# Threshold search on distances, conversion words in PSUM, dummy products in the first choice, three low halves from SBUF

## The chip, the core and the metric

The kernel runs on one core of a Trainium2 chip. The metric is the device time of one execution in microseconds (us). Engines are TensorE (PE; its weight loads are shown as PEld), VectorE (DVE), ScalarE (ACT), GpSimd (POOL) and SyncE (SP).

## The reference

Attention with a gated bias on 4 x 8 heads of 576 x 64, then a layer of eight experts in which the (token, expert) pairs are taken by falling logit until each expert has 288 of the 2304 tokens, then a dense layer with a mish-like activation.

```python
attn_out = _attn_ref(**attn_kwargs)              # causal, bias from a running sum of max(s, 0)
x = attn_out.transpose(0, 2, 1, 3).reshape(B * S, H * D)
logits = x @ w_gate; order = np.argsort(-logits.flatten())
for idx in order:
    tok, e = idx // E, idx % E
    if assigned[tok] >= 0 or counts[e] >= cap: continue
    assigned[tok] = e; counts[e] += 1
out[mask] = np.maximum(x[mask] @ w1[e], 0.0) @ w2[e]      # for each expert e
h = x @ w_in
return ((h * np.tanh(np.log1p(np.exp(h)))) @ w_out).astype(np.float32)
```

`w_in` and `w_out` arrive as 64-bit floats; the kernel reads them as pairs of 32-bit words.

## The kernel before, in words

All products are made in three: each operand is a high part of reduced precision and a low part, the rest.

*Attention* (lines 664 to 1106) works through 224 blocks in a fixed order. `t_unit` transposes queries and keys (a tail of 64 rows at L795), `guard` (L877) bounds the scores, `emit_s` makes scores, `emit_pv` the value products (L983 to L985; key block 4 has 64 rows), and `post_pair` turns results back and adds up the gate logits `L`.

*Conversion* (class `Convert`, from L31). The 64-bit weights of the dense layer come in 64 units of 128 x 256. Each takes three DVE steps that join the two words into one float (L101, L104, L107, one per `yield`), then a high part on ACT (L83) and a low part on POOL (L84). 21 units are converted during attention into tiles that the experts use later, and are split later by `settle`. The others have a tile named `c1` (six buffers), which the activation `mish` shares. `conv(n)` takes n steps.

*The choice* (`route(e)`, L254) finds the expert that is next full and its 288 tokens. `m` is each token's best logit. A threshold is found in six searches, two of 64 candidates and four of 32: a mask on DVE (L263), 18 products that count per expert (L268), a comparison with 288 that counts thresholds (L272), a diagonal (L274) and a product that spreads the counts over all partitions (L276), a maximum (L279), and a few small operations on integer keys for the next candidates (L288 to L309). Then come counts (L328), the expert (L338), ranks (L350, L351), a one-hot per slot (L373), products that gather the token numbers (L378), and an indirect DMA of the tokens (L391). Everything of it that lies in PSUM lies in one bank, `bank` (named `rt` in the trace).

For expert 0 this runs by itself between attention and the experts: at each `yield` the loop at L640 takes conversion steps by the list `BUB`, settles three units, and once the expert is known loads and splits its weights (`feed`, L435: loads by SP, high part on ACT L431, low part on POOL L432). For experts 1 to 7 it runs beside the expert before: `step()`, called after every third product, counts down the number that `route` yielded.

*The experts.* `up(e)` makes 192 products (w1, relu, w2) and `down(e)` 384 on the dense layer, in 16 blocks f. `mish` follows each first-layer product: L555, four ACT operations (L556 to L559), then `product` (L562) four ticks later, ACT (L564), and `low` (L568) one tick later. The product banks `hp` are three; the second layer lags by three blocks. `make_xt` (L489) transposes the gathered tokens. In `up` and `down` one conversion step is taken per tick (two ticks per twelve products) until all are done; `need` takes more if a unit is missing.

```python
    BUB = []
    for T in range(6):
        BUB += [2 if T < 1 else 4 if T < 2 else 2, 1, 2, 0]
    BUB += [2, 3, 2, 0, 1, 0] + [0] * (NT // 6 + 1) + [4]
    BUB9 = 6
```

By these lists the first choice takes 32 steps in its searches, 12 behind them, and 6 before `make_xt(0)`.

Of the kernel before, what the change touches and what calls it, by code (L numbers as in the profile page):

```python
# [27 lines left out]
def fb(ap):  # L28
    return ap.bitcast(F32)


class Convert:


    def __init__(self, nc, w_in, w_out, ring):
# [5 lines left out]
        self.limit, self.loaded, self.done, self.raw, self.held = 0, 0, 0, {}, []  # L41
        self.steps = self.run()
# [47 lines left out]
    def run(self):  # L90
        nc = self.nc
        for i, unit in enumerate(self.units):
# [4 lines left out]
            if self.wide:  # L97
# [6 lines left out]
                nc.vector.scalar_tensor_tensor(a, w[:, :, :, 1], -0x40000000, a, op0=OP.bitwise_and,  # L104
                                               op1=OP.bitwise_or)
                yield
                nc.vector.scalar_tensor_tensor(a, w[:, :, :, 0], 29, a, op0=OP.logical_shift_right,  # L107
# [10 lines left out]
def constants(nc, one, K):  # L118
# [12 lines left out]
    nc.gpsimd.memset(new("onesb", [128, 128], BF16), 1.0)  # L131
    yield
# [21 lines left out]
    jj, th1, j20 = K["jj"], new("th1", [128, 64], I32), new("j20", [128, 64], F32)  # L154
    x1 = j20.bitcast(I32)
    nc.vector.tensor_scalar(th1, jj, -32.0, float(2 ** 26), op0=OP.add, op1=OP.mult)
    yield
    nc.vector.tensor_scalar(x1, th1, 31, 0x7FFFFFFF, op0=OP.arith_shift_right, op1=OP.bitwise_and)
    yield
    nc.vector.tensor_tensor(th1, th1, x1, op=OP.bitwise_xor)  # L160
    yield
    nc.vector.tensor_copy(th1[:, 0:1], th1[:, 1:2])
    yield
    nc.vector.tensor_scalar(j20, jj, float(2 ** 20), None, op0=OP.mult)
    yield
# [45 lines left out]
def experts(ctx, tc, K, ring, ident, L, x_dram, w1, w2, cv, out):  # L211
# [14 lines left out]
    jj, onesb, upper, slots, aux, erow, th1, j20, cb = (K[n] for n in (  # L226
        "jj", "onesb", "upper", "slots", "aux", "erow", "th1", "j20", "cb"))
    steps = K["steps"]
# [4 lines left out]
    diag = one.tile([128, E], F32R, name="diag")  # L233
    nc.gpsimd.memset(fb(diag), 0.0)
# [4 lines left out]
    place = {}  # L239

    def inbank(name, n):
        if name not in place:
            place[name] = place.get("", 144)
            place[""] = place[name] + n
            assert place[""] <= 512
# [899 lines left out]
```

## Time and profile before

| | |
|---|---|
| runs | 1065.06, 1066.26, 1062.24 us; median 1065.06 |
| profiled execution | 1061.81 us, its span 1059.9 us |
| busy | PE 957.4 us (90%), DVE 675.5, ACT 627.7, POOL 437.1 |
| granted PE clock, mean | 0.948 of full speed (2.4 GHz) |
| chain that ended last | PE 62%, DVE 13%, issue 9%, ACT 6%, DMA 5%, POOL 3% |

Busy times are shares of one profiled execution. In a row of the timeline the first number is the start in us from the span's begin, the second the duration; in square brackets stands how long the engine was idle before, and what ended that. "x18" means that so many neighbouring instructions are merged, and the duration is that of all.

### The profile page before, as it was taken

Reading aid. Unit: us, or ns where it says so; the run is one execution under the profiler, and the core shown is the slowest. Engines: PE = TensorE matmul, PEld = TensorE weight load, DVE = VectorE, ACT = ScalarE, POOL = GpSimd, SP = SyncE. Lnnn points to the kernel's source line nnn. Section 1 sums busy time; section 2 is a strip of 40 time slices with the busy share of each in tenths; the row PEclk is TensorE's granted clock in tenths of the full one; section 3 lists DMA queues with packets and bytes.
Section 4 is the critical chain, followed back from the end, with each engine's and each line's share of the span. In section 5 each row is a group of like instructions: output and inputs, shape, how many; then the busy total and the mean of one; then the engine's idle time right before and its main releaser. Section 6 shows DMA issues by size and latency. Waiting matters only on the chain.

```text
span 1059.9 us, 21486 instructions
## 1 busy us (share of the span) xinstructions
PE 957.4 (90%) x7625; PEld 919.4 (87%) x7625; DVE 675.5 (64%) x2041; ACT 627.7 (59%) x1405; POOL 437.1 (41%) x441
## 2 busy tenths in 40 slices
PE   6899988999923879899999999999999999999996
PEld 5788877888812779899998999999999999999996
DVE  7767787997688789746645645655664664443243
ACT  4667765777741357646745664664674565575563
POOL 5546666567665652460251045036035115502401
PEclk8889998999965899999999999999999999999998
DMA  5898999893234534330230123123033023401200
GB/s 131 177 192 194 211 194 204 193 211 96 63 119 140 156 108 127 97 104 1 85 99 22 51 71 86 40 63 103 1 98 108 1 61 98 139 11 30 74 1 23
DMA packets 134580, 105.58 MB, mean 100 GB/s; under 512 B 63977, under 2 KB 114313, under 8 KB 134441
## 3 DMA queue, kind: packets, MB, share of 16 engines
q1 hardware_dynamic: 122520, 83.50, 32.3%
q10 hardware_dynamic: 8880, 11.27, 3.5%
q0 software_dynamic: 3072, 9.44, 2.8%
q8 instruction: 60, 0.98, 0.4%
q14 instruction: 48, 0.39, 0.1%
HBM read 69.55 MB, written 9.73 MB: 75 GB/s over the span
## 4 chain that ended last, share of the span: by engine, by line
PE 62%; DVE 13%; issue 9%; ACT 6%; DMA 5%; POOL 3%; SPq 1%; ACTq 0%; POOLq 0%; DVEq 0%
PE y L462 8%; PE hp L462 8%; PE y L463 7%; PE y L464 7%; PE hp L463 7%; PE hp L464 7%; PE pv L983 2%; PE t L1028 2%; PE s L945 2%; DMA qkraw<-in_k_dram 2%; PE t L877 2%; POOL wt L432 2%; PE pv L985 2%; PE pv L984 1%; PE rt L268 1%
## 5 line engine op out<-in xcount | busy, mean ns | idle before, releaser
L432 POOL TENSOR_TENSOR wt<-raw,wt 128x512 fp32r<-128x512 f32 x128 | 164.2, 1299 | 368.9 <-ACT wt L431 355.3
L962 POOL TENSOR_TENSOR Pl<-P,Ph 128x384 fp32r<-128x384 f32 (+2 forms) x128 | 137.0, 1077 | 98.6 <-DVE Ph L961 45.1
L462 PE MATMUL hp<-xu,WI 128*128 128x288 f32 x512 | 154.5, 302 | 14.8 <-DVE act L568 14.8
L462 PE MATMUL y<-act,WO 128*128 128x288 f32 x512 | 156.6, 306 | 0.0
L464 PE MATMUL hp<-xu,WI 128*128 128x288 f32 x512 | 152.0, 297 | 0.0
L463 PE MATMUL y<-act,WO 128*128 128x288 f32 x512 | 151.9, 297 | 0.0
L464 PE MATMUL y<-act,WO 128*128 128x288 f32 x512 | 151.6, 296 | 0.0
L463 PE MATMUL hp<-xu,WI 128*128 128x288 f32 x512 | 151.1, 295 | 0.4 <-DVE xu L540 0.4
L562 DVE SCALAR_TENSOR_TENSOR hp<-c,hp 128x288 f32<-128x288 f32 x128 | 58.8, 459 | 86.5 <-ACT c L559 85.1
L462 PEld LDWEIGHTS hp<-xu,WI 128*128 128x128 f32 x512 | 96.6, 189 | 16.9 <-DVE act L568 16.9
L431 ACT ACTIVATE wt<-raw 128x512 fp32r<-128x512 f32 x128 | 79.7, 625 | 41.2 <-DMA raw<-in_moe_w_dram 18.0
L463 PEld LDWEIGHTS hp<-xu,WI 128*128 128x128 f32 x512 | 97.1, 190 | 0.9 <-DVE xu L540 0.9
L463 PEld LDWEIGHTS y<-act,WO 128*128 128x128 f32 x512 | 97.6, 191 | 0.0
L464 PEld LDWEIGHTS y<-act,WO 128*128 128x128 f32 x512 | 97.2, 190 | 0.0
L462 PEld LDWEIGHTS y<-act,WO 128*128 128x128 f32 x512 | 97.0, 190 | 0.0
L464 PEld LDWEIGHTS hp<-xu,WI 128*128 128x128 f32 x512 | 96.7, 189 | 0.0
L555 DVE TENSOR_SCALAR c<-hp 128x288 f32<-128x288 f32 x128 | 58.2, 455 | 58.2 <-PE hp L464 46.6
L522 DVE SCALAR_TENSOR_TENSOR act<-hp,act 128x288 fp32r<-128x288 f32 x64 | 29.2, 456 | 101.3 <-ACT act L521 100.6
L556 ACT ACTIVATE c<-c 128x288 f32<-128x288 f32 x128 | 56.7, 443 | 60.2 <-DVE c L555 58.2
L954 ACT ACTIVATE P<-s 128x384 f32<-128x384 f32 (+2 forms) x128 | 63.9, 504 | 40.7 <-PE s L947 23.5
L564 ACT ACTIVATE act<-hp 128x288 fp32r<-128x288 f32 x128 | 52.3, 408 | 60.0 <-DVE hp L562 56.8
L462 PE MATMUL hp<-xu,wt 128*128 128x288 f32 x256 | 80.8, 315 | 1.4 <-ACT xu L499 1.4
(230 smaller groups left out, 2790.1 us busy)
## 6 DMA issues: line engine op xcount, KB each, us to landing
raw<-in_moe_w_dram SPq DMA_DIRECT2D x128, 256.0 KB
QKB<-qk SPq DMA_DIRECT2D x55, 288.0 KB
QKA<-qk SPq DMA_DIRECT2D x29, 288.0 KB
r<-in_moe_w_out_dram ACTq DMA_DIRECT2D x22, 256.0 KB
r<-in_moe_w_in_dram ACTq DMA_DIRECT2D x21, 256.0 KB
qkraw<-in_q_dram SPq DMA_DIRECT2D x32, 128.0 KB
qkraw<-in_k_dram SPq DMA_DIRECT2D x32, 128.0 KB
vraw<-in_v_dram SPq DMA_DIRECT2D x32, 128.0 KB
```

What stands on the lines that cost most here:

```text
L431: nc.scalar.activation(t[:, 0], r, AF.Copy)
L432: nc.gpsimd.tensor_sub(t[:, 1], r, fb(t)[:, 0])
L462: nc.tensor.matmul(out_ap, ah, bh, start=first, stop=False)
L463: nc.tensor.matmul(out_ap, ah, bl, start=False, stop=False)
L464: nc.tensor.matmul(out_ap, al, bh, start=False, stop=last)
L522: nc.vector.scalar_tensor_tensor(h[:, 1], p[:, :CAP], 0.0, fb(h)[:, 0], op0=OP.max, op1=OP.subtract)
L555: nc.vector.tensor_scalar(a, p[:, :CAP], 20.0, None, op0=OP.min)
L556: nc.scalar.activation(a, a, AF.Exp)
L562: nc.vector.scalar_tensor_tensor(p[:, :CAP], a, 0.5, p[:, :CAP], op0=OP.subtract, op1=OP.mult)
L564: nc.scalar.activation(g[:, 0], p[:, :CAP], AF.Copy, scale=-2.0)
L954: nc.scalar.activation(P[:, :n], p[:, :n], AF.Exp, scale=0.125)
L962: nc.gpsimd.tensor_sub(Pl[:, :n], P[:, :n], fb(Ph)[:, :n])
```

## The change

Six edits.

1. The search no longer computes new candidates. `v` is each token's distance from the last threshold found, scaled, and every search compares it with the constants 1, 2, 3 ... (`jj`). Flags are spread over all partitions by one product with 64 columns and counted there (`accum_out`), and one operation gives the next distance. Some waits counted in steps get shorter (leads 10, 16, 8 become 8, 8, 6; 4 becomes 3).
2. The first two conversion steps of a unit write to `cv.temp`, 256 columns of `bank`, from the experts' phase on.
3. `BUB` becomes `[2, 0, 1, 0] * 6 + [1, 0, 0, 1, 0, 0, 0, 0, 0, 2, 0]`: 18 steps in the searches, 4 behind, then 5 before `make_xt(0)`.
4. In the first choice `awake(n)` issues n products of 128 columns into a spare bank, and 40 before and 12 between the transposes of `make_xt(0)`. Before, there were 40 bf16 products ahead of `make_xt(0)`. The first weights are still loaded once the expert is known, but only one is split, and that once the token numbers are known; the rest follow behind `make_xt(0)`. The gather products follow each third of the one-hot.
5. For f < 3 `mish` writes its product to its own SBUF tile instead of the `hp` bank, and ACT and `low` read it there.
6. In attention the 64-row transposes and value products become 128-row ones; 64 rows of `qkraw` are set to zero at the start. Constants no longer used are dropped.

```diff
@@ Convert.run
+                b = a if self.temp is None else self.temp
-                nc.vector.tensor_scalar(a, w[:, :, :, 1], 3, 0x3FFFFFFF, op0=OP.logical_shift_left,
+                nc.vector.tensor_scalar(b, w[:, :, :, 1], 3, 0x3FFFFFFF, op0=OP.logical_shift_left,
...
-                nc.vector.scalar_tensor_tensor(a, w[:, :, :, 0], 29, a, op0=OP.logical_shift_right,
+                nc.vector.scalar_tensor_tensor(a, w[:, :, :, 0], 29, b, op0=OP.logical_shift_right,
@@ route
+    cv.temp = bank[:, 256:512].bitcast(I32).rearrange("p (c f) -> p c f", c=2)
...
+        def search(T, lead):
+            nc.vector.tensor_tensor(mask[:, :, :T], v[:, :, None].to_broadcast([128, NT, T]),
+                                    jj[:, None, :T].to_broadcast([128, NT, T]), op=OP.is_ge)
             yield lead
             for c in range(NT):
+                nc.tensor.matmul(bank[:E, :T], oh[:, c, :], mask[:, c, :T], start=c == 0, stop=c == NT - 1)
             yield 2
-            nc.vector.tensor_scalar(fl[:, 1:T], p[:E, 1:T], CAP - 0.5, None, op0=OP.is_ge, op1=OP.add,
-                                    accum_out=n)
-            nc.vector.tensor_scalar(diag[:E], identp[:E], n, None, op0=OP.mult)
-            yield 4
-            nc.tensor.matmul(p[:, 64:64 + E], onesF, diag, start=True, stop=True)
+            nc.vector.tensor_scalar(flags[:E, :T], bank[:E, :T], CAP - 0.5, None, op0=OP.is_ge)
+            yield 3
+            nc.tensor.matmul(bank[:, 64:64 + T], onesF, flags[:, :T], start=True, stop=True)
             yield 2
-            J = inbank("J", 1)
-            nc.vector.tensor_reduce(J, p[:, 64:64 + E], axis=AX.X, op=OP.max)
+            nc.vector.tensor_scalar(fl[:, 1:T], bank[:, 65:64 + T], 0.5, None, op0=OP.is_ge, op1=OP.add,
+                                    accum_out=J)
...
+            yield from search(64, 8)
+            nc.vector.tensor_scalar(v, v, R["J"], -1.0, op0=OP.subtract, op1=OP.max)
+            nc.vector.tensor_scalar(v, v, 1.0, 32.0, op0=OP.min, op1=OP.mult)
+            nc.vector.tensor_tensor(v, v, lf, op=OP.add)
+            for i in range(4):
+                yield from search(32, 6)
+                nc.vector.tensor_scalar(v, v, R["J"], 32.0 if i < 3 else 1.0, op0=OP.subtract, op1=OP.mult)
...
             yield 3 if c + 6 < NT else 8
+            if e == 0:
+                gather_slots(range(c, c + 6))
@@ mish
+        u = a if f < 3 else p[:, :CAP]
...
-            nc.vector.scalar_tensor_tensor(p[:, :CAP], a, 0.5, p[:, :CAP], op0=OP.subtract, op1=OP.mult)
+            nc.vector.scalar_tensor_tensor(u, a, 0.5, p[:, :CAP], op0=OP.subtract, op1=OP.mult)
-            nc.scalar.activation(g[:, 0], p[:, :CAP], AF.Copy, scale=-2.0)
+            nc.scalar.activation(g[:, 0], u, AF.Copy, scale=-2.0)
@@ first choice
+    def awake(n):
+        for _ in range(n):
+            nc.tensor.matmul(spare[:64, 0:128], upperF[:, :64], onesF, start=True, stop=True)
+
+    for i, _ in enumerate(route(0)):
+        conv(BUB[i] if i < len(BUB) else 0)
         cv.settle(3)
+        if i < 24:
+            awake((0, 5, 0, 14)[i % 4])
+        else:
+            awake(8)
+        if (0, "ei") in R and at["load"] < NRAW:
+            feed(0)
+        if (0, "ei") in R and (0, "idx") in R and at["split"] < 1:
             feed(1)
+    cv.settle(99)
+    conv(5)
+    awake(40)
+    make_xt(0, range(NJ), 12)
     feed()
@@ attention
+        nc.vector.memset(qkraw[i][64:128, :, 4], 0.0)
...
-                nc.tensor.transpose(p[:, 64 * t:64 * t + 64], qkraw[pr][:64, t, 4], ident[:64, :64])
+                nc.tensor.transpose(p[:, 128 * t:128 * t + 128], qkraw[pr][:, t, 4], ident)
...
-        ph, pl = Ph[:m, at:at + n], Pl[:m, at:at + n]
-        nc.tensor.matmul(o, VH[i][:m, a, hs], ph, start=first, stop=False)
+        ph, pl = Ph[:, at:at + n], Pl[:, at:at + n]
+        nc.tensor.matmul(o, VH[i][:, a, hs], ph, start=first, stop=False)
```

## Rows read from the trace of the kernel before

**Rows 1.** Stretches; columns: length, busy us (x) of each engine, PEclk, DMA, GB/s.
```profile
296.06:329.14 33.08, 7.10 (x114) 5.76 (x114) 31.08 (x86) 10.48 (x31) 24.09 (x31) 0.51 0.37 112
329.14:351.60 22.46, 8.75 (x74) 7.66 (x74) 19.23 (x53) 6.05 (x13) 12.34 (x13) 0.58 0.63 184
351.60:388.20 36.60, 33.00 (x249) 32.02 (x250) 28.71 (x70) 14.61 (x33) 23.45 (x22) 0.86 0.44 132
388.20:452.10 63.90, 57.34 (x476) 55.41 (x475) 53.58 (x163) 44.51 (x107) 20.92 (x24) 1.00 0.34 102
452.10:481.10 29.00, 29.00 (x264) 28.85 (x263) 14.25 (x44) 12.00 (x25) 18.18 (x18) 1.00 0.34 95
481.10:538.50 57.40, 55.59 (x476) 55.21 (x475) 35.20 (x112) 38.74 (x90) 8.01 (x7) 1.00 0.17 48
```

**Rows 2.** Waits of PE, 424 us to the end: total, times, longest (us).
```profile
PE hp L462 <- DVE act L568: 12.6, 8, 1.8
```

**Rows 3.** The stretch view over most of attention, columns as in rows 1.
```profile
40.00:240.00 200.00, 185.38 (x1272) 166.10 (x1271) 159.70 (x557) 136.09 (x301) 117.10 (x113) 0.94 0.91 198
```

**Rows 4.** Timeline of expert 7's down stage, around its fourth product.
```profile
1000.85 0.46 DVE L562 SCALAR_TENSOR_TENSOR hp<-c,hp 128x288 f32<-128x288 f32 x1 [0.36 <-ACT c L559]
...
1003.42 0.40 PE L462 MATMUL hp<-xu,WI 128*128 128x288 f32 x1 [1.84 <-DVE act L568]
```

**Rows 5.** Timeline of expert 1's down stage, the same place.
```profile
574.15 0.45 DVE L562 SCALAR_TENSOR_TENSOR hp<-c,hp 128x288 f32<-128x288 f32 x1
...
575.59 0.40 PE L462 MATMUL hp<-xu,WI 128*128 128x288 f32 x1 [1.74 <-DVE act L568]
```

**Rows 6.** POOL's weight subtraction in 481 to 540 us: min/median/max ns, first and last start.
```profile
L432 POOL TENSOR_TENSOR wt<-raw,wt x4: 1288/1297/1317, 517.5 to 529.5; 128x512 fp32r<-128x512 f32 x4
```

**Rows 7.** Groups by line on DVE, 296 to 352 us: count, busy, mean ns, idle before.
```profile
L107 DVE SCALAR_TENSOR_TENSOR c<-r,c 128x256 int32<-128x256 int32 x16 | 13.8, 864 | 0.4
L104 DVE SCALAR_TENSOR_TENSOR c<-r,c 128x256 int32<-128x256 int32 x17 | 9.8, 577 | 0.4
L101 DVE TENSOR_SCALAR c<-r 128x256 int32<-128x256 int32 x17 | 7.3, 430 | 0.2 <-DMA r<-in_moe_w_in_dram 0.2
L263 DVE TENSOR_TENSOR mask<-rt,th 128x576 fp32r<-128x576 f32 x4 | 3.0, 757 | 0.1
```

**Rows 8.** Timeline between the first choice and expert 0's first product.
```profile
345.34 4.46 DVE L107 SCALAR_TENSOR_TENSOR c<-r,c 128x256 int32<-128x256 int32 x1
...
351.60 0.61 PE L462 MATMUL hp<-xu,wt 128*128 128x288 f32 x1 [1.37 <-ACT xu L499]
```

**Rows 9.** Timeline of the gather products in the first choice.
```profile
337.39 2.07 DVE L373 TENSOR_TENSOR mask<-slots,rt 128x576 bf16<-128x576 f16 x3
...
338.19 0.15 PEld L378 LDWEIGHTS <-mask 128*96 128x96 bf16 x1 [3.09 <-DVE mask L373]
...
339.52 1.53 PE L378 MATMUL rt<-aux,mask 128*96 128x6 bf16 x18 [4.30 <-DVE idf L383]
```

**Rows 10.** Timeline of a narrow search in the first choice.
```profile
325.84 0.65 PE L268 MATMUL rt<-mask,oh 128*8 128x32 f32 x18 [2.41 <-DVE mask L263]
...
326.82 0.17 DVE L272 TENSOR_SCALAR_CACHE_REDUCE fl<-rt 8x31 bf16<-8x31 f32 x1
...
327.30 0.38 PE L276 MATMUL rt<-diag,onesF 128*128 128x8 f32 x1 [0.82 <-DVE diag L274]
```

**Rows 11.** Waits of PE's weight loads, 352 to 392 us, as in rows 2.
```profile
PEld rt L276 <- DVE diag L274: 3.9, 2, 3.4
```

**Rows 12.** Timeline of value products on 64 rows in attention, and the product behind.
```profile
78.10 0.27 PE L984 MATMUL pv<-Ph,VL 64*128 64x64 f32 x1
78.21 0.27 PE L985 MATMUL pv<-Pl,VH 64*128 64x64 f32 x1
78.42 0.42 PE L945 MATMUL s<-QKB 128*128 128x320 f32 x1
```

**Rows 13.** Timeline of the start: the memset behind which the added ones stand.
```profile
2.09 2.08 DVE L712 MEMSET QKA<- 5x2432 f32 x1 [0.55 <-issue]
```

More of the change, by code (lines that the diff above doesn't have):

```diff
@@ L232, in experts, with inbank @@
     nc.vector.tensor_copy(upperF, upper)
-    diag = one.tile([128, E], F32R, name="diag")
-    nc.gpsimd.memset(fb(diag), 0.0)
+    flags = one.tile([128, 64], F32R, name="flags")
+    nc.gpsimd.memset(fb(flags), 0.0)
     R = {}
     bank = ps_r.tile([128, 512], F32, name="rt")
[L239 to L245, printed above, removed]
-        return bank[:, place[name]:place[name] + n]
-    identp = inbank("identp", E)
-    nc.vector.tensor_copy(identp[:E], ident[:E, :E])
+    place = dict(m=(144, NT), v=(162, NT), cnt=(180, E), se=(188, E), low=(196, NT), high=(214, NT),
+                 sl=(196, 2 * NT), jg=(196, 2 * NT), pt=(196, NT), pe=(214, E), sr=(232, NT), idp=(250, NJ))
+    def inbank(name):
+        at, n = place[name]
+        return bank[:, at:at + n]
+    cv.temp = bank[:, 256:512].bitcast(I32).rearrange("p (c f) -> p c f", c=2)
     def small(shape, dt, name, bufs=2):
@@ L322, in route @@
-        ge = inbank("ge", NT)
-        nc.vector.tensor_scalar(ge, m, lam, None, op0=OP.is_ge)
+            ge = v
+            nc.vector.tensor_scalar(ge, m, NEG / 16, None, op0=OP.is_ge)
+        else:
+            sign = small([128, NT], I32, "sign", 1)
+            nc.vector.tensor_scalar(sign, m.bitcast(I32), 31, 0x7FFFFFFF, op0=OP.arith_shift_right,
+                                    op1=OP.bitwise_and)
+            key, low, high = inbank("sr").bitcast(I32), inbank("low"), inbank("high")
+            nc.vector.tensor_tensor(key, m.bitcast(I32), sign, op=OP.bitwise_xor)
+            nc.vector.tensor_scalar(high.bitcast(I32), key, 20, 0x4B000800, op0=OP.logical_shift_right,
+                                    op1=OP.bitwise_xor)
+            nc.vector.tensor_scalar(v, high, -float(2 ** 23), 2.0 ** -6, op0=OP.add, op1=OP.mult)
+            first = search(64, 8)
+            n = next(first)
+            nc.vector.tensor_scalar(low.bitcast(I32), key, 0xFFFFF, 0x4B000000, op0=OP.bitwise_and,
+                                    op1=OP.bitwise_or)
+            lf = small([128, NT], F32, "lf", 1)
+            nc.vector.tensor_scalar(lf, low, -float(2 ** 23), 2.0 ** -15, op0=OP.add, op1=OP.mult)
+            yield n
+            yield from first
+            nc.vector.tensor_scalar(v, v, R["J"], 64.0, op0=OP.subtract, op1=OP.mult)
+            yield from search(64, 8)
[5 more added lines that the diff above has]
+                nc.vector.tensor_scalar(v, v, R["J"], 32.0 if i < 3 else 1.0, op0=OP.subtract, op1=OP.mult)
+            ge = m
+            nc.vector.tensor_scalar(ge, v, 0.0, None, op0=OP.is_ge)
@@ L371, in route, with gather_slots @@
         ohs = small([128, NT, JW], BF16, "mask", 1)
+        def gather_slots(cs):
+            for c in cs:
+                nc.tensor.matmul(bank[:JW, 0:2 * NJ], ohs[:, c], aux[:, c].rearrange("p j w -> p (j w)"),
+                                 start=c == 0, stop=c == NT - 1)
         for c in range(0, NT, 6):
@@ L487, in experts, with make_xt @@
     XT = {}
-    def make_xt(e, parts=range(NJ)):
+    def make_xt(e, parts=range(NJ), between=0):
         for j in parts:
@@ L500, in make_xt @@
             nc.vector.tensor_sub(xt[:, 1, :, js], src, fb(xt)[:, 0, :, js])
+            if between:
+                awake(between)
     def hl(t):
```

134 lines of the change are left out of this document (27 added, 107 removed).

## The prediction

> **What bounds the kernel now.** I read the page first: its slices show TensorE (PE) busy nearly throughout, except in a valley between attention and the experts. The stretch table then puts sizes on the stages [rows 1]. From 296.06 to 351.60 us, 55.5 us, the first expert choice runs alone: PE works 7.10 of its first 33.08 us at half clock, while DVE is busy 31.08. This stage is a DVE chain. Expert 0 follows: 36.6 us up and 63.9 us down, against 29.0 and 57.4 in expert 1, so it carries 14.1 us too much, with DVE busy 28.71 and 53.58. From expert 1 on PE is the bound, with one hole per expert: a wait of up to 1.8 us on the low half of the first sum [rows 2]. Attention is bound by PE and DMA in turn: PE 185.4 of 200 us, DMA share 0.91 [rows 3].
>
> The sum is made against the profiled execution, 1061.8 us (span 1059.9). The median of the runs is 3.2 above it, and I add that at the end.
>
> **1. Low halves of three sums, once per expert.** A product bank is free for the fourth product (f=3) only when L568 has read it. Now L562 writes its result to SBUF for f<3, so the bank is free when L562 ends. In expert 7 L562 ends at 1001.31; PE starts at 1003.42, after a wait of 1.84, once the low half is there [rows 4]. All of that wait goes, but then the twelve products of f=3 end by about 1003.2 to 1003.4 (384 products fill 57.4 us in expert 1, so twelve take at most 1.8 [rows 1]), and the second layer's first products need the low half of 1003.4: gain 1.5. In expert 1 L562 ends at 574.60 and PE starts at 575.59 [rows 5]: gain 0.95, since a search mask stands ahead of L562 in DVE's queue. Seven experts route the next choice beside their sums and are of the second kind: 7 x 0.95 + 1.5 = 8.2. The new order of the search can move the mask away, so I take **-8.5**; ends -12 (no mask ahead in any: 8 x 1.5) and -5.
>
> L568 now has two SBUF inputs. In expert 1's down stage POOL runs nothing before 517.5 us [rows 6], 30 us after these three. The Trainium skill (SBUF — State Buffer, Who interferes with whom) says a VectorE instruction with two SBUF inputs contends with a GpSimd instruction that reads SBUF, and whoever is second waits for the whole of it. By that rule alone each low half could wait one POOL instruction, and the -8.5 would be near zero; the row shows POOL empty there, so I keep it.
>
> **2. Conversion words in PSUM.** A unit is three DVE steps, L101, L104, L107. In the first choice they average 430, 577 and 864 ns, 0.54 without the one of 4.46 us [rows 7, 8]. No row shows the new form (one SBUF operand, the rest in PSUM); the nearest is L562 [rows 4], SBUF and PSUM to PSUM, 0.46 for 288 columns, so 0.43 for 256 and 0.47 with the gap to the next. Bounds 0.40 and 0.55.
>
> The price is the bank. The words lie in the bank of the routing products. In [rows 9] the first gather product has its weights at 338.19 but starts at 339.52, just as the third mask ends (337.39 + 2.07), although it needs only the first mask; the others merely read another part of that bank. So products and DVE accesses of this bank wait for each other whatever the columns, and conversion steps that ran beside the search products now stand in line with them.
>
> **3. The search itself (first choice).** Before, six searches with 32 conversion steps and what leads in took 33.1 us [rows 1]. New narrow search: mask 0.76, two steps 0.94, 18 products 0.65 plus 0.15 for hand-offs (an estimate), flags 0.21 (as L272, 0.17, plus a gap), one step 0.47, spreading product 0.38 plus 0.15, and count and distance 0.25 each, estimated from L272 too [rows 10]: 4.2 us. A wide one has twice the mask and 0.1 more of product: 5.0. Six: 4 x 4.2 + 2 x 5.0 = 26.8. Around them stand some eleven small operations at about 0.2, 2.2: 29.0. **-4.1**. If the steps did not wait for the products, about 0.9 less each: -9.5. At 0.55 a step, for 18 steps: -2.7.
>
> Dummy products stand in PE's queue while DVE works: at the clock's lower level, 1.2 GHz, 128 columns are 0.11 us (an estimate), and 14 x 0.11 = 1.5 fall beside count, distance, mask and two steps (2.2 in all), 5 x 0.11 beside flags and step (0.7). They cost nothing while DVE is later; if DVE were quicker than I think, up to 0.5 per search.
>
> **4. From the searches to expert 0's first product.** Before, 22.5 us [rows 1]. Seven conversion steps stood around the count and the pick, some five on the path (5 x 0.58 = 2.9, the mean with a gap [rows 7]); now 1 + 1 + 2 behind the gather, all in line, 4 x 0.47 = 1.9: -1.0. The gather in three groups alternates with the masks that read the same bank, so it stays a sum: 0. Behind the indices, one L107 sat 4.46 us on DVE (345.34 to 349.80) and held the scalar engine's split, and so its copies of the first tokens until after the last rows had come; product one started at 351.60 [rows 8]. Now only one weight split is ahead, five cheap steps run meanwhile, and two of three copies are done early, at full clock: -1.5, ends 0 and -3. Together **-2.5**. The splits held back are due at PE's pace: one POOL subtraction, about 1.3 us [rows 6], per 12 products, up to 1.8.
>
> **5. Expert 0.** Up: clock 0.86 over 36.6 us means 0.28 x 36.6 = 10 us at half clock [rows 1]; dummies keep PE warm into it, and I estimate that over half of these 10 us come first: -2.5. DVE stalled the spreading product 3.9 us [rows 11], behind slow conversion steps: -2. Back come waits of routing products for a step just queued: +1. **-3.5**, ends -7 and +3. Down: 27 steps were done before expert 0 instead of 50, so 23 x 0.47 = 10.8 us of DVE work comes in here, less some 79 x 0.08 = 6.3, as the 79 others get cheaper. DVE was 84% busy in the down stage (53.58 of 63.9), so half of the net 4.5 shows: **+2**, ends -3 and +8.
>
> **6. Later experts' choices.** Three DVE operations fewer per search on an engine that is not the bound: nothing. But a mask's products come 6 PE steps after it instead of 8, and flags to spreading 3 instead of 4: two searches per expert in the down stage, 0.1 each on average: **+1**, ends 0 and +4.
>
> **7. Attention.** Products on 64 rows become products on 128. Leaving a group of 64 rows takes 0.21 (78.21 to 78.42), against 0.11 between two of its products [rows 12]: 0.1 for leaving, and I take the same for entering, which could be nothing. 32 value groups and 16 transpose pairs at 0.2: 9.6 us of PE, at least 4.8. In 40 to 240 us DMA is 0.91 busy [rows 3] and takes back what it can; I take under half, **-4**, ends 0 and -9. Two added memsets of 256 elements on DVE, by 2.08 us for 2432 [rows 13], 0.2 each, ahead of the bias chain: +0.4, or nothing if they fit in the 0.55 idle before that row. **-3.6** net. The constants dropped ran off the path.
>
> **Sum:** -8.5 - 4.1 - 2.5 - 3.5 + 2 + 1 - 3.6 = -19.2. 1061.8 - 19.2 = 1042.6, and with 3.2 for the median **1045.8**, about 1046.
>
> **Rivals.** *(a) More:* the steps do not wait for the products (-5.4 more), attention gives all (-5): 1035. For it: each is one exclusion away; against: [rows 3, 9]. *(b) Less:* only the sums' hole closes for sure, and what the searches gain comes back in expert 0, whose DVE gets 23 more steps: 1065 - 8.5 - 3 = 1053.5. For it: DVE's 84%; against: its steps cost less. *(c) Slower:* the shared bank in expert 0. PE's queue is in order, and each routing group (12 in searches, 4 behind) waits for the conversion step last queued on DVE, which itself stands behind a wait for the scalar engine. If each of 16 costs PE 2 us, 32 us come back and the total is 1046 + 32 - 1 = 1077. It decides from an average of 1.3 us per group. For it: the one wait of 3.4 [rows 11]; against: conversion steps are queued several products ahead. The Trainium skill (PSUM — Partial Sum Buffer, PSUM bank collisions raise a hardware error) asks that any two engines on one bank and quadrant be kept apart, columns or not; [rows 9] agree. *(d) Not what it says:* POOL meets the low halves, DMA binds attention throughout: 1065 - 6 = 1059 to 1063.
>
> **How the numbers follow.** Forecast 0.55 (1038 to 1051), (a) 0.17 (1026 to 1038), (b) 0.18 (1051 to 1059.5), (c) 0.04, (d) 0.06. Range 1030 to 1057, which leaves out some 2 in 10. About 0.5% (1059.7 and 1070.4) is what a measurement of this kernel can tell from no change: faster 0.90, same 0.06, slower 0.04.
>
> **What would show it.** PE's waits on L568 at the fourth product gone or under 0.5 us; conversion steps at 0.42 to 0.46 whatever POOL does; a search of 4.2 us with PE's 18 products starting only after the second step; clock near 1.00 from 300 us on; expert 0 up near 33, down near 64.5; attention ending 3 to 5 us sooner. Wrong would make it: steps above 0.55, PE waits over 1 us on conversion lines in expert 0, or a first choice of over 52 us.

## The result: slower, and where the time went

The changed kernel takes 1071.07 us (median of 18 runs, 1066.96 to 1078.13), the kernel before 1064.84 (18 runs, 1058.46 to 1072.46): a ratio of 1.0060, with a 95% interval of 1.0038 to 1.0081. The forecast was 1046, its range 1030 to 1057. The profiled execution of the changed kernel is the longest of its 18, 1078.13 us with a span of 1076.4. The stages below are read from it, against the 1059.9 of before. Its 7 us above the median are not in experts 1 to 7, which take 588.9 to 589.3 us in all twelve profiled kernels built on the changed one; some 2 us may be attention's (see below), and the rest may lie in the first choice or expert 0.

The stretch view of the changed kernel: first choice, expert 0 up and down, expert 1 up and down. Columns as in [rows 1].

```profile
295.04:349.02 53.98, 38.16 (x432) 35.00 (x432) 34.58 (x113) 13.87 (x39) 25.34 (x36) 0.67 0.34 102
349.02:394.12 45.10, 35.93 (x270) 33.94 (x270) 24.61 (x71) 15.15 (x34) 25.75 (x25) 0.83 0.42 123
394.12:479.12 85.00, 67.66 (x455) 64.50 (x456) 59.86 (x171) 47.38 (x115) 25.80 (x32) 0.86 0.34 101
479.13:509.47 30.34, 29.87 (x282) 29.47 (x281) 14.77 (x45) 12.10 (x25) 18.12 (x18) 1.00 0.31 90
509.47:564.87 55.40, 54.83 (x457) 54.50 (x456) 32.16 (x98) 38.36 (x90) 7.96 (x7) 1.00 0.17 50
```

Between the same marks in both kernels (start of attention's last six products, first product of each expert, end of the last product of all): those six start 1.85 us later (295.04 against 293.19); the first choice falls from 58.4 (the prediction's 55.5 counts from 296.06) to 54.0; expert 0 rises from 100.5 to 130.1; experts 1 to 7 fall from 599.5 to 589.0; what follows the last product takes 8.3 in both. That is 1.85 - 4.43 + 29.62 - 10.51 = 16.53, the whole difference of the spans. The first choice and experts 1 to 7 went the way that was forecast; expert 0 took back about twice what these two gave. [Rows 1] have its stretches of before: 36.60 up and 63.90 down, clocks 0.86 and 1.00. Now they are 45.10 and 85.00 at 0.83 and 0.86, with DVE less busy in the up stage than before (24.61 against 28.71).

What PE waits for in expert 0 of the changed kernel, 349.02 to 479.12 us (total, times, longest). L103, L106 and L109 are the three conversion steps, L84 and L85 their unit's splits:

```profile
PE rt L241 <- DVE rt L106: 6.3, 4, 3.8
PE hp L427 <- ACT WI L84: 6.0, 2, 4.2
PE rt L335 <- DVE c L109: 3.5, 1, 3.5
PE rt L245 <- DVE rt L103: 2.7, 4, 1.3
PE rt L287 <- DVE rt L106: 1.9, 1, 1.9
PE rt L310 <- DVE rt L103: 1.6, 1, 1.6
PE hp L429 <- POOL WI L85: 1.3, 1, 1.3
PE rt L241 <- DVE rt L103: 1.1, 2, 0.6
```

Two kinds stand here, and the same view of before (351.60 to 452.10 us) has neither. Routing products (tile rt) wait for conversion steps: these lines and one of 0.6 make 17.7 us in 14 waits. And the first layer's products (hp) wait for converted weights themselves, 7.3 us. The first kind speaks for the shared bank (the prediction's rival c), the second for the 23 conversion steps that the change leaves over for expert 0. The experiments part the two.

### The profile page after: what moved, and what is told of

It is laid out like the page before. It is cut to its first block, busy times and chain, and to the rows that moved or that the text cites. A ratio compares the mean times of both kernels' runs of the same rounds, so it can differ in the third digit from the quotient of the medians.

```text
span 1076.4 us, 21912 instructions
## 1 busy us (share of the span) xinstructions
PE 981.3 (91%) x7863; PEld 947.1 (88%) x7863; DVE 644.6 (60%) x1941; ACT 625.5 (58%) x1405; POOL 430.6 (40%) x440
## 4 chain that ended last, share of the span: by engine, by line
PE 47%; issue 6%; DVE 3%; ACT 1%; POOL 1%; DMA 0%; POOLq 0%; DVEq 0%; ACTq 0%
PE y L427 8%; PE hp L427 7%; PE y L429 7%; PE y L428 7%; PE hp L429 7%; PE hp L428 7%; PE rt L241 1%; DVE mask L237 1%; POOL wt L397 1%; PE hp L461 1%; PE hp L588 1%; PE rt L335 1%; DVE c L518 0%; POOL out_dram L597 0%; DMA raw<-in_moe_w_dram 0%
## 5 line engine op out<-in xcount | busy, mean ns | idle before, releaser
L427 PE MATMUL hp<-xu,WI 128*128 128x288 f32 x512 | 157.0, 307 | 10.0 <-ACT WI L84 6.0
L429 PE MATMUL hp<-xu,WI 128*128 128x288 f32 x512 | 154.3, 301 | 1.3 <-POOL WI L85 1.3
L428 PE MATMUL hp<-xu,WI 128*128 128x288 f32 x512 | 151.9, 297 | 0.1
L527 DVE SCALAR_TENSOR_TENSOR hp<-c,hp 128x288 f32<-128x288 f32 x104 | 47.9, 460 | 105.4 <-ACT c L522 105.4
L427 PEld LDWEIGHTS hp<-xu,WI 128*128 128x128 f32 x512 | 98.4, 192 | 12.2 <-ACT WI L84 6.5
L396 ACT ACTIVATE wt<-raw 128x512 fp32r<-128x512 f32 x128 | 79.7, 624 | 45.7 <-PE y L429 20.3
L429 PEld LDWEIGHTS hp<-xu,WI 128*128 128x128 f32 x512 | 98.3, 192 | 1.8 <-POOL WI L85 1.8
L428 PEld LDWEIGHTS hp<-xu,WI 128*128 128x128 f32 x512 | 98.8, 193 | 0.4 <-DVE xu L507 0.3
L428 PEld LDWEIGHTS y<-act,WO 128*128 128x128 f32 x512 | 98.2, 192 | 0.6 <-DVE act L533 0.6
L429 PEld LDWEIGHTS y<-act,WO 128*128 128x128 f32 x512 | 98.5, 192 | 0.0
L427 PEld LDWEIGHTS y<-act,WO 128*128 128x128 f32 x512 | 98.5, 192 | 0.0
L356 POOL DMA_INDIRECT xg<-x_dram,idx x24 | 22.5, 939 | 185.8 <-DVE rt L362 180.7
L529 ACT ACTIVATE act<-hp 128x288 fp32r<-128x288 f32 x104 | 42.7, 411 | 70.1 <-DVE hp L527 64.0
```

The source lines that it names most:

```text
L396: nc.scalar.activation(t[:, 0], r, AF.Copy)
L427: nc.tensor.matmul(out_ap, ah, bh, start=first, stop=False)
L428: nc.tensor.matmul(out_ap, ah, bl, start=False, stop=False)
L429: nc.tensor.matmul(out_ap, al, bh, start=False, stop=last)
L527: nc.vector.scalar_tensor_tensor(u, a, 0.5, p[:, :CAP], op0=OP.subtract, op1=OP.mult)
L529: nc.scalar.activation(g[:, 0], u, AF.Copy, scale=-2.0)
```

## Experiments

Theories: **bank** (the conversion words lie in the bank of the routing products, so each waits for the other) and **postponed steps** (27 conversion steps run ahead of expert 0 instead of 50, and expert 0 pays for the rest). Ratios are to the kernel before on the same chip. Stages are those of the profiled execution, in us, between the marks given above; the last column is DVE's busy time in expert 0. Two pairs give an idea of how well a stage repeats: before, x_low_only and x_att_only have the same first choice (58.4 each), and x_no_temp and x_no_awake the same expert 0 but for the clock that they bring along (121.2 and 122.4).

| kernel | median | ratio (95%) | first choice | expert 0 up + down | DVE |
|---|---|---|---|---|---|
| before | 1064.8 | | 58.4 | 36.6 + 63.9 | 82.3 |
| changed | 1071.1 | 1.006 (1.004 to 1.008) | 54.0 | 45.1 + 85.0 | 84.5 |
| x_no_temp | 1057.8 | 0.991 (0.988 to 0.995) | 44.4 | 39.5 + 81.7 | 97.2 |
| x_bub_old | 1064.4 | 0.9995 (0.998 to 1.001) | 62.1 | 41.0 + 69.3 | 75.7 |
| x_both | 1050.0 | 0.984 (0.976 to 0.992) | 56.8 | 37.4 + 64.1 | 82.5 |
| x_temp_only | 1078.1 | 1.010 (1.002 to 1.019) | 64.5 | 36.0 + 71.6 | 78.1 |
| x_own_bank | 1053.5 | 0.987 (0.979 to 0.996) | 42.2 | 39.5 + 80.5 | 96.2 |
| x_no_awake | 1056.3 | 0.988 (0.980 to 0.997) | 45.4 | 39.6 + 82.8 | 97.7 |
| x_low_only | 1056.7 | 0.990 (0.986 to 0.994) | 58.4 | 36.6 + 63.5 | |
| x_att_only | 1064.7 | 0.999 (0.996 to 1.002) | 58.4 | 36.4 + 64.4 | |
| x_own_51 | 1048.4 | 0.983 (0.979 to 0.987) | 50.5 | 39.5 + 66.4 | 84.4 |
| x_own_39 | 1051.6 | 0.986 (0.983 to 0.990) | 49.3 | 39.5 + 73.0 | 91.3 |
| x_pace | 1047.7 | 0.983 (0.979 to 0.986) | 42.6 | 45.8 + 69.5 | 98.5 |
| x_old_search | 1053.4 | 0.989 (0.985 to 0.993) | 53.2 | 39.9 + 65.1 | 84.2 |
| x_less_dve | 1037.9 | 0.977 (0.974 to 0.979) | 41.3 | 30.2 + 70.6 | 61.1 |
| x_tail39 | 1049.4 | 0.987 (0.984 to 0.989) | 45.7 | 39.8 + 73.0 | 90.8 |
| x_tail75 | 1055.1 | 0.992 (0.989 to 0.994) | 61.8 | 39.8 + 62.8 | 72.5 |

### Bank and postponed steps, singly and together

x_no_temp: the changed kernel with the words in SBUF.

```diff
-    cv.temp = bank[:, 256:512].bitcast(I32).rearrange("p (c f) -> p c f", c=2)
```

> The changed kernel with the conversion's words in SBUF again; all else as changed (27 steps ahead of expert 0). It tells two theories of the 29.6 us that expert 0 gained (100.5 to 130.1 us) apart. Bank: the conversion steps and the routing products of expert 1's choice share a PSUM bank and wait for each other by turns; then PE's waits on conversion lines go and expert 0 comes back to 100 to 112 us, the total to 1045 to 1057. Postponed steps: 23 conversion steps more fall due in expert 0 and come in bursts ahead of the sums; then expert 0 stays at 120 us or more, and the total at 1066 to 1085, since the steps are dearer in SBUF. The first choice should lengthen by up to 9 us in both, if POOL slows the steps as it did before.

x_bub_old: the changed kernel with the old list of steps.

```diff
-    BUB = [2, 0, 1, 0] * 6 + [1, 0, 0, 1, 0, 0, 0, 0, 0, 2, 0]
+    BUB = []
+    for T in range(6):
+        BUB += [2 if T < 1 else 4 if T < 2 else 2, 1, 2, 0]
+    BUB += [2, 3, 2, 0, 1, 0] + [0] * (NT // 6 + 1) + [4]
...
-    conv(5)
+    conv(6)
```

> The changed kernel with the old count of conversion steps ahead of expert 0 (50 instead of 27), the words still in PSUM. Postponed steps: expert 0 falls to 100 to 108 us, the first choice grows by 23 x 0.47 = 11 us, and the total is 1052 to 1060. Bank: expert 0 still holds 79 steps against 102 in the same bank, so it stays at 118 us or more, and the total is 1068 or more.

x_both: both edits.

> The changed kernel with the words in SBUF and the old 50 conversion steps ahead of expert 0. If bank and postponed steps are two separate causes, they add: expert 0 from 130.1 less 8.9 (words in SBUF) less 19.8 (old count) to about 101, the first choice from 54.0 less 10.4 plus 8 to about 52, the total about 1044 to 1050. If they are one cause (the steps hurt only because they stand in the bank, or the bank only because more steps meet it), the second remedy adds little to the first: expert 0 stays at 108 or more and the total at 1053 or more.

Neither theory alone held, and the first two expectations each missed a half: with the words in SBUF expert 0 stays at 121.2, and with the old count it falls to 110.3, but not to 100. The four kernels make a square. In expert 0, taking the bank away gives 130.1 - 121.2 = 8.9 and 110.3 - 101.5 = 8.8 us; not postponing gives 19.8 and 19.7. They are two causes, and over the whole of expert 0 they add. Taken by themselves its two stages do not quite: the bank is worth 5.6 and 3.6 us in the up stage, 3.3 and 5.2 in the down stage. In the first choice taking the bank away gives 9.6 and 5.3 us, while postponing saves 8.1 (bank shared) or 12.4 (not shared). So over both stages postponing costs a net 7.3 to 11.7 us by the traces, 7 to 8 by the ratios; the bank costs 14.1 to 18.5 by the traces, 15 to 17 by the ratios. I had expected the bank's price in the first choice to have the other sign: the steps are cheaper in PSUM, and the stage is longer all the same. In x_both the expectation held for expert 0 (101.5) and the total, but not for the first choice, 56.8 instead of 52.

x_temp_only: the kernel before, with the words moved into the routing bank and nothing else (the bank's small tiles are put together to make room).

```diff
+    cv.temp = bank[:, 256:512].bitcast(I32).rearrange("p (c f) -> p c f", c=2)
...
-                nc.vector.tensor_scalar(a, w[:, :, :, 1], 3, 0x3FFFFFFF, op0=OP.logical_shift_left,
+                b = a if self.temp is None else self.temp
+                nc.vector.tensor_scalar(b, w[:, :, :, 1], 3, 0x3FFFFFFF, op0=OP.logical_shift_left,
```

> The kernel before with one part of the change alone: the conversion's words in the bank of the routing products. The prediction's steps 2 and 3: steps at 0.43, a first choice shorter by a few us, expert 0 shorter by about 2, total 1058 to 1063. The bank theory after the first runs: the routing products of the first choice and of expert 0 stand in line with the steps, first choice 3 to 10 us longer, expert 0 5 to 12 us longer, total 1070 to 1085.

Alone on the kernel before, too, it costs: first choice +6.1, expert 0 +7.1. PE's largest waits there are on the steps again (357.79 to 465.39 us; L268, L276, L350 and L378 are routing products of the old search):

```profile
PE rt L268 <- DVE rt L106: 2.7, 3, 1.3
PE rt L276 <- DVE rt L106: 2.6, 3, 1.2
PE rt L378 <- DVE c L109: 2.1, 1, 2.1
PE rt L350 <- DVE rt L106: 2.0, 1, 2.0
```

### PSUM, or the sharing?

x_own_bank: in the first choice the words lie in a bank that nothing else uses then; from expert 0 on, where all eight banks are taken, in SBUF.

```diff
-    cv.temp = bank[:, 256:512].bitcast(I32).rearrange("p (c f) -> p c f", c=2)
...
     spare = ps_y.tile([128, 512], F32, name="y")
+    words = ps_y.tile([128, 512], F32, name="y")
+    cv.temp = words[:, :256].bitcast(I32).rearrange("p (c f) -> p c f", c=2)
...
     conv(5)
+    cv.temp = None
```

> The changed kernel with the words in PSUM during the first choice, but in a bank that holds nothing else then, and in SBUF from expert 0 on; 27 steps ahead as changed. Sharing theory: steps at 0.42 us and the 18 search products no longer behind the second step, so a narrow search takes 2.5 to 3.2 us (3.93 with the shared bank, 3.18 with SBUF), the first choice 38 to 44 us, expert 0 as with SBUF, 121, the total 1052 to 1058. PSUM theory (words in PSUM are slow for the chain wherever they lie): a narrow search at 3.7 us or more, the first choice 50 us or more, the total 1064 or more.

A narrow search in the timeline of the changed kernel (start, us, engine, line):

```profile
314.47 0.76 DVE L237 TENSOR_TENSOR mask<-rt,jj 128x576 fp32r<-128x576 f32 x1
315.26 0.43 DVE L103 TENSOR_SCALAR rt<-r 128x256 int32<-128x256 int32 x1
315.72 0.43 DVE L106 SCALAR_TENSOR_TENSOR rt<-r,rt 128x256 int32<-128x256 int32 x1
316.20 0.65 PE L241 MATMUL rt<-mask,oh 128*8 128x32 f32 x18 [0.71 <-DVE rt L106]
316.89 0.18 DVE L243 TENSOR_SCALAR flags<-rt 8x32 fp32r<-8x32 f32 x1 [0.74 <-PE rt L241]
317.00 0.40 DVE L109 SCALAR_TENSOR_TENSOR c<-r,rt 128x256 int32<-128x256 int32 x1
317.45 0.39 PE L245 MATMUL rt<-flags,onesF 128*128 128x32 f32 x1
...
318.39 0.76 DVE L237 TENSOR_TENSOR mask<-rt,jj 128x576 fp32r<-128x576 f32 x1
```

The same in x_own_bank, whose line numbers are one lower here:

```profile
307.50 0.76 DVE L236 TENSOR_TENSOR mask<-rt,jj 128x576 fp32r<-128x576 f32 x1
308.17 0.42 DVE L103 TENSOR_SCALAR y<-r 128x256 int32<-128x256 int32 x1
308.31 0.64 PE L240 MATMUL rt<-mask,oh 128*8 128x32 f32 x18 [0.48 <-DVE mask L236]
308.62 0.43 DVE L106 SCALAR_TENSOR_TENSOR y<-r,y 128x256 int32<-128x256 int32 x1
308.98 0.18 DVE L242 TENSOR_SCALAR flags<-rt 8x32 fp32r<-8x32 f32 x1
309.09 0.42 DVE L109 SCALAR_TENSOR_TENSOR c<-r,y 128x256 int32<-128x256 int32 x1
309.22 0.28 PE L244 MATMUL rt<-flags,onesF 128*128 128x32 f32 x1
...
310.05 0.76 DVE L236 TENSOR_TENSOR mask<-rt,jj 128x576 fp32r<-128x576 f32 x1
```

The same operations at the same cost take 3.92 us from mask to mask in the one and 2.55 in the other. With the shared bank the 18 products start at the end of the second step, and DVE waits 0.74 for them; the spreading product starts at the end of L109. With a bank of their own the products start at the end of the mask and run beside the steps. With the words in SBUF the search took 3.18, though L106 and L109 are then 0.83 us each. So it is the sharing and not PSUM: 1.37 us in each narrow search.

### The dummy products

x_no_awake: x_no_temp without the dummies between the steps of the first choice.

```diff
-        if i < 24:
-            awake((0, 5, 0, 14)[i % 4])
-        else:
-            awake(8)
```

> The changed kernel with the words in SBUF and without the dummy products between the steps of the first choice (those just ahead of the first tokens' transposes stay). If the dummies raise the granted clock, the clock of the first choice stays at 0.50 here (0.78 and 1.00 from 310 us on with them), the 18 products of a narrow search take 0.64 at half clock throughout, and expert 0 starts 2 to 5 us later and at half clock: total 1060 to 1065 against 1057.8. If they do nothing, or cost as much as they bring, 1056 to 1059.

Stretches of x_no_temp, then of x_no_awake (columns as in [rows 1]):

```profile
305.00:310.00 5.00, 4.54 (x52) 4.16 (x51) 4.76 (x15) 2.44 (x8) 5.00 (x8) 0.50 0.16 52
310.00:315.00 5.00, 4.14 (x67) 3.54 (x66) 4.86 (x13) 0.42 (x1) 5.00 (x7) 0.78 0.37 106
315.00:320.00 5.00, 3.87 (x62) 3.44 (x62) 4.79 (x15) 0.84 (x2) 5.00 (x7) 1.00 0.19 55
```

```profile
310.00:315.00 5.00, 2.00 (x38) 1.55 (x38) 4.86 (x13) 0.42 (x1) 5.00 (x7) 0.50 0.33 98
315.00:320.00 5.00, 1.53 (x20) 1.10 (x20) 4.67 (x15) 0.83 (x2) 5.00 (x7) 0.50 0.30 89
```

The dummies do raise the granted clock, from 0.50 (1.2 GHz) to 1.00 (2.4 GHz). It brings 1.0 us in the first choice (45.4 against 44.4), where DVE is busy nearly throughout (4.67 to 4.86 of 5.00 us in these rows), and nothing in expert 0's up stage (39.6 against 39.5). The expected loss of 2 to 5 us in the total isn't there: the two ratios cannot be told apart. In the changed kernel the same dummies run, but the clock stays at 0.50 up to 330 us:

```profile
310.00:315.00 5.00, 3.79 (x46) 3.43 (x46) 3.53 (x12) 0.83 (x3) 5.00 (x8) 0.50 0.25 70
325.00:330.00 5.00, 5.00 (x46) 4.83 (x45) 3.08 (x14) 0.42 (x1) 0.73 (x1) 0.50 0.20 56
```

The dummies stand in PE's queue behind routing products that now wait for DVE. That this is why the clock came late is argued, not shown.

### The low halves and attention, each alone on the kernel before

x_low_only:

```diff
+        u = a if f < 3 else p[:, :CAP]
...
-            nc.vector.scalar_tensor_tensor(p[:, :CAP], a, 0.5, p[:, :CAP], op0=OP.subtract, op1=OP.mult)
+            nc.vector.scalar_tensor_tensor(u, a, 0.5, p[:, :CAP], op0=OP.subtract, op1=OP.mult)
```

> The kernel before with one part of the change alone: the product of the first three sums of every expert is written to SBUF, and the low half read from there. The prediction's term: -8.5 us (ends -12 and -5), a ratio of 0.992; the trace of the changed kernel says about -8 (down stages of experts 1 to 7 shorter by 2 each, with up stages that also changed). If POOL met the two SBUF operands, no change.

x_att_only: attention's part of the diff (128 rows, two memsets).

> The kernel before with one part of the change alone: attention's last 64 rows taken as 128 rows with zeros, and the two memsets. The prediction's term: -3.6 us (ends -9 and +0.8). The trace of the changed kernel, whose last attention product comes 1.25 us later, says 0 to +2: DMA, or work elsewhere, sets attention's pace.

The low halves give 10.3 us by the ratio, and 11.0 by the traces (experts 1 to 7: 599.5 to 588.5). Of [rows 2], 12.6 us on L568, this is left from expert 1 on, on the product L564 (L562 of before):

```profile
PE hp L462 <- DVE c L564: 4.1, 5, 0.9
```

Attention alone gives 1 us at best estimate, and the interval (-3.8 to +1.9) takes in both no change and the predicted -3.6. Its end moves about: its last six products start at 290.0 to 295.0 in the thirteen profiled kernels with 128 rows, at 293.2 to 299.0 in four with 64 rows. The means, 292.6 and 295.6, lean to the prediction, but settle nothing.

### What postponed steps cost, and how

x_own_39 and x_own_51 are x_own_bank with 39 and 51 steps ahead of expert 0; x_pace leaves 27 ahead but takes them faster in its up stage; x_old_search is the kernel before with the low halves, 51 steps and the words in their own bank in the first choice.

```diff
-    BUB = [2, 0, 1, 0] * 6 + [1, 0, 0, 1, 0, 0, 0, 0, 0, 2, 0]
+    BUB = [3, 1, 1, 0] * 6 + [1, 0, 0, 1, 0, 0, 0, 0, 0, 2, 0]
```

and in x_pace:

```diff
-    side = {"route": None, "at": 0, "next": 0, "conv": (1, 1), "up": True}
+    side = {"route": None, "at": 0, "next": 0, "conv": (2, 1), "up": True}
```

> Words in a PSUM bank of their own during the first choice (in SBUF from expert 0 on), and 51 conversion steps ahead of expert 0 instead of 27, in the old places. Both theories of the first runs: expert 0 at about 101 us as in the kernel with both remedies, the first choice 42.2 plus 24 steps of which half show, 47 to 52 us, total 1040 to 1048, under every kernel so far.

> As the one before, but 39 steps ahead of expert 0: two more in each search than the 27 of the change. It tells two forms of the theory of postponed steps apart. Due times: 63 steps in attention, 39, 31 in expert 0's up stage and 4 per sum in its down stage stay ahead of the 12 per sum that fall due, up to the last sum, where with 27 the last two sums force a burst of 3 and one of 8 steps; so no burst is left and expert 0 takes 100 to 105 us, as with 50 ahead. DVE's capacity: the cost is proportional to the steps moved into expert 0, 12 of 23 come back, and expert 0 takes 108 to 113 us. First choice 43 to 47 us; total 1038 to 1046 or 1046 to 1052.

> Words in their own bank, 27 steps ahead of expert 0 as in the change, but in expert 0's up stage two steps and one by turns instead of one each time: 15 of the steps come earlier within expert 0, none leaves it. Due times: no burst is left at the last two sums, the down stage falls from 80.5 us to 62 to 67, the up stage grows by up to 4, expert 0 takes 102 to 108 us, total 1038 to 1045. DVE's capacity: the sum of the work is the same, expert 0 stays at 115 us or more, total 1050 or more.

> The kernel before (its search, its order, its attention, no dummies) with two parts: the low halves of three sums from SBUF, and the words in a PSUM bank of their own during the first choice, with 51 steps ahead of expert 0. Against the changed kernel with the same two things it gives what the new search, the dummies and the new order of the first choice are worth: by the prediction's steps 3 to 5, with cheap steps on both sides, 5 to 12 us, so a first choice of 52 to 57 us here and 1046 to 1053 in all; if the new search is worth nothing by itself, the first choice is 47 to 52 us and the total 1040 to 1047.

The theory of due times missed: 112.5 us with 39 steps (100 to 105 expected), 115.4 with the earlier pace (102 to 108). x_own_39's first choice, 49.3, missed as well (43 to 47), and so did x_own_51's expert 0: 105.9 where 101 was expected. It is 4.4 above x_both's, and x_old_search's, 105.0, is 4.9 above x_low_only's, though from expert 0 on each pair differs in nothing but one step more ahead, 51 against 50. With 27 ahead the bank of the first choice makes no such difference (120.0 against 121.2). 27 and 51 are whole units of three steps and 50 is not, so where in a unit expert 0 begins may be worth 4 to 5 us; no run tests it. Then I took DVE's work for the bound, since its busy share of expert 0 is 0.80 to 0.82 in before, x_no_temp, x_both and the x_own kernels alike, and took work away from it:

```diff
 # x_less_dve
-                nc.vector.scalar_tensor_tensor(b, w[:, :, :, 1], -0x40000000, b, op0=OP.bitwise_and,
-                                               op1=OP.bitwise_or)
+                if i < 30:
+                    nc.vector.scalar_tensor_tensor(b, w[:, :, :, 1], -0x40000000, b, op0=OP.bitwise_and,
+                                                   op1=OP.bitwise_or)
```

(and so the third step). x_tail39 and x_tail75 have 39 and 75 steps ahead, more of them behind the searches and between the tokens' transposes.

> Words in their own bank and 27 steps ahead, as before; in expert 0 the second and third conversion step of each of its 34 units are left out (so the converted words of those units are not the reference's), while loads, splits on ACT and POOL, and the times at which units fall due stay. Expert 0 was 120.0 us with DVE busy 96.2. DVE's work as the bound: 34 x (0.535 + 0.571) = 37.6 us of DVE work go; at the share of 0.80 seen in all kernels with words in SBUF, (96.2 - 37.6) / 0.80 = 73 is under what PE needs, so PE sets it: 85 to 95 us, total 1020 to 1030. Due times, or the latency of load, split and subtraction: nothing of these is taken away, expert 0 stays at 108 us or more, total 1041 or more.

> Words in their own bank; 39 steps ahead of expert 0, the 12 beyond the 27 put where DVE waits in the first choice: 5 behind the count, rank and gather products, 7 between the indices and the last tokens. DVE's work as the bound of expert 0: 112.5 us as with the other 39; first choice 42.2 plus 0 to 2, since those places were idle; total 1042 to 1047. If DVE is not idle there in effect (its steps hold up the tokens' low halves), the first choice is 45 us or more and the total 1048 or more.

> As the one before with 75 steps ahead of expert 0. A step exposed in the first choice costs 0.42 us, one left for expert 0 0.57 / 0.80 = 0.7. DVE's work as the bound: expert 0 has 48 steps fewer than with 27, 96.2 - 48 x 0.57 = 69 us of DVE work, and is set by PE: 86 to 94 us; first choice 42 plus 36 x 0.42 = 57, up to 60; total 1036 to 1043. If expert 0 keeps 100 us or more, its length hangs on something other than DVE's work and the total is 1050 or more.

That theory missed as well: 100.8 and 102.6 us, where 85 to 95 was expected. Each theory has a part of it, and the stages go some way to tell them apart. Expert 0's stretches in x_own_bank, then in x_less_dve (up, down):

```profile
332.20:371.70 39.50, 31.74 (x271) 29.86 (x269) 30.33 (x71) 15.01 (x35) 26.52 (x25) 0.96 0.48 140
371.70:452.20 80.50, 65.65 (x455) 62.03 (x456) 65.88 (x170) 47.18 (x115) 26.42 (x32) 0.87 0.35 106
```

```profile
334.77:364.99 30.22, 29.05 (x272) 28.32 (x270) 18.76 (x52) 16.14 (x36) 26.24 (x25) 1.00 0.60 184
364.99:435.57 70.58, 61.46 (x457) 59.45 (x456) 42.37 (x122) 45.77 (x114) 25.43 (x31) 0.90 0.40 121
```

**Up:** without two of three steps it takes 30.2 us, what expert 1 takes. So 9.3 us of it go with DVE's work. They don't depend on how many steps ran ahead (39.5 to 39.8 with 27, 39, 51 and 75; x_both with 50 has 37.4): the up stage takes one step at each of 31 places whatever is left. With 15 more, x_pace, it takes 6.3 us more. **Down:** 80.5, 73.0, 66.4 and 62.8 us with 27, 39, 51 and 75 ahead. PE's waits on the splits of converted weights (L84, L85) fall from 9.9 to 4.1 to none to none. The granted clock is 0.87 with 27 and 0.92 with 51, whose down stage is this:

```profile
382.56:448.95 66.39, 60.41 (x455) 58.81 (x456) 53.05 (x147) 44.42 (x107) 20.70 (x24) 0.92 0.33 97
```

Taken over PE's busy time, the clock loses some 0.13 x 65.65 = 8.5 us with 27 ahead and 0.08 x 60.41 = 4.8 with 51. From 27 to 51 the stage falls by 14.1 us; the waits and the clock make 9.9 + 3.7 = 13.6. These rows of x_own_bank are the whole of the waits on splits (371.70 to 452.20 us):

```profile
PE hp L426 <- ACT WI L84: 7.5, 3, 4.8
PE hp L428 <- POOL WI L85: 2.4, 2, 1.5
```

The two longest stand ahead of the first products of the last two sums, and behind each the clock falls; it is 1.00 from 412 to 428 us, and again from 446 on. Two rows of the timeline, then two stretches:

```profile
427.96 0.40 PE L426 MATMUL hp<-xu,WI 128*128 128x288 f32 x1 [2.40 <-ACT WI L84]
440.40 0.61 PE L426 MATMUL hp<-xu,WI 128*128 128x288 f32 x1 [4.80 <-ACT WI L84]
```

```profile
428.00:436.00 8.00, 6.69 (x24) 5.59 (x24) 4.52 (x10) 2.82 (x7) 2.07 (x3) 0.57 0.41 121
439.00:446.00 7.00, 5.60 (x22) 5.22 (x23) 3.32 (x8) 2.11 (x5) 2.07 (x3) 0.52 0.24 75
```

A third fall, at 404.8 to 411.6 us, stands behind a routing wait of 3.7. So postponed steps come due at the last sums, PE stops there for weights, and the clock falls behind the holes. The changed kernel against x_bub_old gives the same picture with other weights. x_bub_old's expert 0 (up, down):

```profile
354.44:395.45 41.01, 31.73 (x271) 29.88 (x269) 25.55 (x71) 16.48 (x36) 26.15 (x25) 0.96 0.46 135
395.45:464.76 69.31, 59.46 (x457) 57.39 (x456) 50.13 (x148) 44.63 (x107) 20.27 (x24) 0.95 0.32 93
```

It has no wait on splits, against 7.3 us; the clock, reckoned as above, loses 4.2 us of PE's busy time against 15.6. That makes 18.7 of the 19.8. 4.8 of the clock's part fall in the up stage, where no product waits for a split, so why they go with postponing is not shown.

My count of due times was too kind: it looked at when a step is queued, not at when the step and the splits behind it are done, so 39 ahead were not enough. That DVE's load makes them late is only part of it: in x_less_dve, with DVE busy 42.37 of 70.58 us instead of 65.88 of 80.50, the waits on splits are still 7.1 us. Its down stage is 9.9 us shorter all the same: the waits on splits give 2.8 of that, those of routing 2.5 (3.9 to 1.4), and the clock, at 0.90, some 2.4. Nor were steps free in places where DVE had waited: x_tail39's first choice is 3.5 us longer for 12 of them, and in x_tail75 the first product waits 7.2 us for the last tokens behind eight of them.

x_old_search against x_own_51, on the same chip, gives the worth of the new search, dummies, order and attention together with the bank out of the way: 1053.4 - 1048.4 = 5 us, though the intervals of the two ratios overlap. The first choice gives 2.7, expert 0 nothing; in the traces attention ends 4.5 us sooner, no more than it differs among kernels with the same attention (290.0 to 295.0). x_pace and x_own_51 are the best versions, 1.7% under the kernel before.

## Why the prediction was wrong, step by step

- **Step 5, expert 0, failed.** It was to give 1.5 us and cost 29.6. "Back come waits of routing products for a step just queued: +1" was 8.9 us. It stood in the up stage alone; of the 17.7 us of such waits 9.0 came in the down stage, where the sum had no term for them. The price of the shared bank was seen [rows 9] and rival (c) named its place, PE in-order behind DVE, but it got 4 in 100 on the ground that steps are queued several products ahead. They are; but DVE, with 82% of expert 0 [rows 1], comes to them late, as the waits show: the longest are 3.8 and 3.5 us, where the prediction had named over 1 us as a sign that it is wrong. The rival's size, 32 us from 2 us in each of 16 groups, is near to what came (29.6) by luck: the waits on steps were 14 of 1.3 us, and x_no_temp shows that PE still waits 9.9 us for routing's own DVE operations when the bank is free. The larger part was the other term: "half of the net 4.5 shows: +2" was 19.8 us. I weighed 23 steps as DVE's busy time spread over the stage. They were not spread: those that came due at the last sums held PE up, and the clock fell behind the holes. The gain for the up stage from a warm PE, -2.5, did not come either: in the changed kernel the clock there is 0.83, under the 0.86 of before, and in x_no_temp and x_no_awake, where it is 0.96 and 1.00, the stage takes 39.5 and 39.6 us all the same.
- **Steps 2 and 3, words and search.** A step at 0.43 was right (0.40 to 0.43), a narrow search of 4.2 was 3.93, and that the products would start only behind the second step was right as well. What failed was to set the cheap steps against the old dear ones and call the search a gain: in SBUF, with steps of 0.83, it is 3.18. I put the wait at 0.9 a search and booked it; its worth against x_own_bank is 1.4. The Trainium skill (PSUM — Partial Sum Buffer, PSUM bank collisions raise a hardware error) asks for two engines on one bank to be kept apart by order, columns or not. The runs agree on the order: words in columns 256 to 511 and products in 0 to 143 take turns.
- **Step 1, low halves:** right in mechanism, small in size: -8.5 against -10.3 (ratio) or -11.0 (traces), within its ends. Their two SBUF inputs cost nothing from expert 1 on (0.458 us a piece); in expert 0, where POOL is busy, one of the three took 0.756 and the others 0.45.
- **Step 4:** with step 3, -6.6 was forecast and -4.4 came, the first product at 349.02, at half clock again. Without the bank the first choice gains 14.0 (x_no_temp), but 12.4 of that are the 23 postponed steps: x_both, which takes the old 50, gains 1.6.
- **Step 6:** +1 was forecast; experts 1 to 7 take 589.0 here, and 588.5 and 587.7 in x_low_only and x_old_search, which have the old search and the low halves: +0.5 to +1.3.
- **Step 7, attention:** -3.6 is neither borne out nor excluded.

By the sum: -19.2 was forecast and +16.5 came in the profiled executions, a miss of 35.7 (25 by the medians). Step 5 is off by 29.6 + 1.5 = 31.1 of it, attention by some 5, steps 3 and 4 by 2; experts 1 to 7 came out 3 better than steps 1 and 6 say.

Still open: how the cost of postponing parts between late weights and the clock behind them, which move together in these runs (the account above only adds them up); where in a unit expert 0 should begin; and whether words in a bank of their own would pay in expert 0, where no bank is free (not tried).

## What to carry to other kernels

A scratch tile put into a bank that another engine's chain uses is not free, however short its instructions: before moving it, list the chain's operations on that bank and give each a turn behind the other engine's last queued one. When work is put off, don't weigh it as a busy share of the later stage; count where it falls due, through every queue that it still has to pass, and who stands still there. And try a change's parts in a square before judging them: here the words in PSUM and the postponed steps hid a search, a set of sums and cheap steps that together make the kernel 1.7% faster (x_own_51), the sums alone 1.0%.

## What the runs showed of the hardware

- Two users of different columns of one PSUM bank took strict turns: 2.55 us a search apart, 3.92 together. Whether the chip or the program's own ordering asks for it, the trace, which shows it as waits, doesn't tell.
- A conversion step with its words in PSUM takes 0.40 to 0.43 us whatever POOL does; in SBUF the same L106 and L109 took 0.42 when POOL was idle and 0.83 to 0.85 beside its subtractions.
